# A linear-attention and expert-routing kernel: three double-bank PSUM buffers for the tile products, one bank shared by three small products, and a new set of step ranks

## The chip, the cores and the metric

The kernel runs on one core of one Trainium2 chip. The metric is the device time of one launch in microseconds (us). Before the change the median of three runs is 548.88 us.

## The reference, cut to what matters

Linear attention over 8 batches of 8 heads, 576 rows and 64 columns is followed by a norm over each head, a router of two levels (4 groups of 4 experts) and, for every one of the 4608 tokens, two matrix products by the one expert that was chosen.

```python
kv  = np.einsum('bhsd,bhse->bhde', k, v)
out = np.einsum('bhsd,bhde->bhse', q, kv)
rms = np.sqrt(np.mean(out * out, axis=-1, keepdims=True) + 1e-06)
x   = (out / rms * g_norm)          # then (4608, 512)
g_idx = np.argmax(x @ w_group, axis=1)
for g in range(4):                  # xg: the tokens of group g
    e_idx = np.argmax(xg @ w_expert[g], axis=1)
    for e in range(4):
        h  = np.maximum(xg[mask_e] @ w1[g, e], 0.0)
        ye = h @ w2[g, e]
        out[tok_idx] = (g_w * e_w)[:, None] * ye
```

## The kernel before, in words

The program has two stages. The first takes the queries, keys and values, makes the attention's output and sorts its rows by expert into a table in device memory (`xs`). The second takes the experts one after the other, largest first, in `for r in range(1, NE)`; the diff does not touch it.

The first stage works on 8 batches. For a batch b SyncE loads keys, values and queries (1 MB each; the last 64 rows of two batches come together as a "tail" of 256 KB). TensorE makes the state of a batch in `kv_product` (tile `kps`, line L567): 32 instructions for the main rows and 8 for the tail. Two copies take it out of PSUM (`kvd`, L555). `wide_product` multiplies it by the router's columns (tile `eps_`, L582, 8 instructions), and two copies put the result into `kvx` (L555), the widened state. From it `o_product` makes one tile of 128 rows at a time (tile `ops`, L615, two PSUM banks): four tiles for each batch and one tail tile for each two batches, 36 tiles, called c0 to c35 below; c31 to c34 are the last batch's and c35 is the last tail. ScalarE copies each tile out in two pieces (`o_keep`, `logits_keep`) and squares it. The tiles fall into 8 groups (of 3, 5, 5, 5, 6, 6, 4 and 2). When a group is complete, a chain of some 25 small VectorE steps (`route`) finds each token's expert. A product in the middle of that chain (tile `rk`, L834 to L840) counts the tokens before it; two VectorE steps read it (`kr` L846 and, in some groups, `lo` L1005). GpSimd then scatters the rows to `xs`.

After the fifth group the fullest expert is known well enough that work for it begins before the stage ends (`early_products`): for two blocks of 128 tokens, j = 0 and 1, a transpose (tile `xtr`, L1184), four pairs of layer-1 products (tile `l`, L369, n = 0 to 3), whose results ScalarE and VectorE split (`hhi` L1208, `hlo` L1214), and three passes of layer 2 (L1238) for each half hf of the output. The product `rv` (L1094) orders the experts once the last group is counted. Three of the four layer-2 sums, (j, hf) = (0,0), (0,1) and (1,0), are made here, and (1,1) opens the second stage.

What sets the order: every piece of work is a `step` with an engine, a rank and the steps that it needs. `give_out` lets each engine take, of the steps that can start by its own reckoning, the one of lowest rank. So each engine's instructions stand in a fixed order, which the tables at the top of the file (RANK, ROUTE, FOLD, LOADS, QLOADS, KVS, TAILS) shift. Where that reckoning leaves TensorE idle early on, `keep_warm` puts in products whose result nobody reads (tile `warm`, L463).

PSUM has eight banks. Before the change `kps`, `rk`, `eps_` (with `rv`) and the spare bank of `early_products` (with `warm`) have one each, and the tile products two buffers of two banks:

```python
ps_k = ph.enter_context(tc.tile_pool(name="ps_k", bufs=1, ...))
ps_r = ph.enter_context(tc.tile_pool(name="ps_r", bufs=1, ...))
ps_t = ph.enter_context(tc.tile_pool(name="ps_t", bufs=1, ...))
ps_e = ph.enter_context(tc.tile_pool(name="ps_e", bufs=1, ...))
ps_o = ph.enter_context(tc.tile_pool(name="ps_o", bufs=2, ...))
```

Of the kernel before, what the change touches and what calls it, by code (L numbers as in the profile page):

```python
# [9 lines left out]
F32 = mybir.dt.float32  # L10
# [30 lines left out]
RANK = {'wl0': 8653.7, 'wl3': -1621.61, 'hl': -1311.21, 'wh': -1318.76, 'wd': 837.56, 'ek': -5681.71, 'o': 3012.77, 'ok': -2407.34, 'sq': -1243.18, 'red': -1306.22, 'w': -1292.39, 'wl': 1177.39, 'wl2': -1202.9, 'xt': -7928.83, 'xs': -1359.19, 'l1': -1645.21, 'hs': -3081.53, 'l2': 3844.97, 'l3': -1942.42, 'l4': -2933.95, 'lk': -12.71, 'rd': -5685.6, 'l0': -1223.92, 'xp': 848.81}  # L41
ROUTE = [251.18, -2343.82, 3560.04, 792.99, -725.82, -1903.73, -9207.47, -3358.1]
FOLD = [242.46, -1256.85, -816.36, -1306.91, -3093.22, 8651.96, -1200.27, 1075.03]
LOADS = [-4110.76, -3081.87, -3084.03, -1307.74, -7.22, 49.97, 846.24, 4399.02]
QLOADS = [-2437.19, -1943.92, -1317.97, -1274.11, 651.34, 665.74, 1915.97, 6713.18]
KVS = [-2548.6, -1773.86, 3654.53, -1443.46, -3012.94, -39.98, -1312.76, -7927.08]
TAILS = [-3374.12, -1314.27, 191.74, -1649.28]
# [19 lines left out]
BIG = 11  # L67
CUT = 5

@with_exitstack  # L70
def tile_linattn_moe(ctx: ExitStack, tc: tile.TileContext, qm, qt, k, v, router, w1, w2, out):
# [345 lines left out]
    with ExitStack() as ph:  # L417
# [159 lines left out]
        def wide_product(b):  # L577
            kv["e"] = ps_t.tile([P, 512], F32, name="eps_", tag="pst")
# [21 lines left out]

        def o_product(c):
# [9 lines left out]
            ps = ps_o.tile([P, 2, 512], F32, name="ops", tag="pso")  # L611
# [84 lines left out]
        def tile_steps(c, nq):  # L696
# [3 lines left out]
            done["o", c] = step("PE", 1.24, c + RANK["o"], rdy + [get("o", c - 1), get("lk", c - 2)],  # L700
# [17 lines left out]
        def route(g):  # L718
# [45 lines left out]
            def f():  # L764
                nc.vector.scalar_tensor_tensor(out=tl([H], "nwy"), in0=v["nwa"], scalar=1.5, in1=v["y"], op0=ALU.add,
                                               op1=ALU.mult)
                v["rinv"] = v["nwy"].rearrange("p (t h) -> p t h", h=H)
# [961 lines left out]
```

## Time and profile before

| what | value |
|---|---|
| median of 3 runs | 548.88 us (548.83 to 552.87) |
| profiled execution, its own time | 550.13 us |
| span of the profile | 548.4 us, so 1.73 us lie outside of it |
| mean granted TensorE clock | 0.991 |
| TensorE busy in the span | 527.0 us (96%) |
| first stage, to the first product of (1,1) | 131.9 us |
| moved by DMA in the span | 126.27 MB |

PE is TensorE's matmul, PEld its weight loads, DVE is VectorE, ACT ScalarE, POOL GpSimd and SP SyncE. A line number is one of the kernel before. An fp32 product shows as two matmuls in the trace for one instruction in the program. PEclk is the clock that TensorE was granted, as a share of 2.4 GHz; 0.50 is 1.2 GHz. In a list of waits, "issue" means that the engine waited for nothing that the profile shows.

### The profile page before, as it was taken

To read this page: it belongs to the slowest core of one execution; us is meant where nothing else is said; L and a number is where in the kernel's file an instruction comes from. 1 tells how busy PE (TensorE), PEld (TensorE's weight loads), DVE (VectorE), ACT (ScalarE), POOL (GpSimd) and SP (SyncE) were. 2 spreads that over 40 slices of the span, in tenths; PEclk is the share of its full clock that TensorE was granted. 3 is DMA by queue.
4 is the path that set the end of the run, shared out by engine and by line. 5 is a ranking of instruction groups with operands and counts; after the bars stand their busy time and mean duration, and the time that the engine had idled before them with its cause. 6 is when DMAs were issued, how large, how long until landed. Compare 5 with 4: busy or idle time off the path is not lost.

```text
span 548.4 us, 11978 instructions
## 1 busy us (share of the span) xinstructions
PE 527.0 (96%) x4416; PEld 509.4 (93%) x4420; DVE 379.6 (69%) x800; ACT 275.2 (50%) x497; POOL 255.2 (47%) x244
## 2 busy tenths in 40 slices
PE   7999898988999999999999999999999999999994
PEld 5788787888999999999999999999999999999994
DVE  4158489792698777877676767776777778787750
ACT  1298487741554454545454545455454645455530
POOL 4001444663221146574746464645564554656543
PEclk9999799999999999999999999999999999999999
DMA  8999997566989373625855656474828474672001
GB/s 333 402 414 408 420 419 291 201 226 205 313 332 333 84 290 113 249 108 148 306 228 171 236 163 248 153 266 136 328 75 328 132 296 182 217 262 102 24 29 41
DMA packets 43631, 126.27 MB, mean 230 GB/s; under 512 B 6767, under 2 KB 25643, under 8 KB 32692
## 3 DMA queue, kind: packets, MB, share of 16 engines
q1 hardware_dynamic: 35732, 105.98, 53.3%
q0 software_dynamic: 7696, 19.48, 9.4%
q8 instruction: 35, 0.57, 0.4%
q14 instruction: 24, 0.20, 0.1%
q10 hardware_dynamic: 144, 0.04, 0.0%
HBM read 106.01 MB, written 20.38 MB: 230 GB/s over the span
## 4 chain that ended last, share of the span: by engine, by line
PE 88%; DMA 3%; SPq 2%; another core or an unknown queue 2%; issue 2%; ACT 1%; POOL 0%; POOLq 0%; ACTq 0%
PE ps L380 12%; PE ps L385 12%; PE ps L381 12%; PE psy L385 11%; PE psy L381 11%; PE psy L380 11%; PE ops L615 6%; PE l L369 3%; PE kps L567 3%; DMA tail_v<-in_v_dram 2%; SPq L542 2%; PE l L1238 1%; PE ps L369 1%; DMA tail_k<-in_k_dram 1%
## 5 line engine op out<-in xcount | busy, mean ns | idle before, releaser
L1417 POOL DMA_INDIRECT out_dram<-z,idx x138 | 166.2, 1204 | 169.1 <-DVE hhl L345 65.2
L385 PE MATMUL ps<-xh,wlo 128*128 128x364 f32 (+14 forms) x480 | 143.2, 298 | 0.0
L381 PE MATMUL ps<-xl,whi 128*128 128x364 f32 (+14 forms) x480 | 143.0, 298 | 0.0
L380 PE MATMUL ps<-xh,whi 128*128 128x364 f32 (+14 forms) x480 | 143.0, 298 | 0.0
L381 PE MATMUL psy<-hhl,w2h 128*128 128x364 f32 (+13 forms) x448 | 134.6, 300 | 0.0
L385 PE MATMUL psy<-hhl,w2l 128*128 128x364 f32 (+13 forms) x448 | 134.6, 300 | 0.0
L380 PE MATMUL psy<-hhl,w2h 128*128 128x364 f32 (+13 forms) x448 | 134.1, 299 | 0.0
L270 DVE TENSOR_TENSOR wlo<-wr,whi 128x1024 fp32r<-128x1024 f32 x64 | 90.7, 1418 | 24.2 <-ACT whi L266 24.1
L354 ACT CAST w2h<-wr 128x1024 fp32r<-128x1024 f32 x60 | 62.6, 1044 | 63.0 <-PE psy L381 44.2
L344 ACT ACTIVATE hhl<-ps 128x364 fp32r<-128x364 f32 (+14 forms) x120 | 50.5, 420 | 79.9 <-PE ps L385 74.6
L380 PEld LDWEIGHTS ps<-xh,whi 128*128 128x128 f32 x480 | 90.4, 188 | 0.0
L381 PEld LDWEIGHTS ps<-xl,whi 128*128 128x128 f32 x480 | 90.3, 188 | 0.0
L385 PEld LDWEIGHTS ps<-xh,wlo 128*128 128x128 f32 x480 | 90.3, 188 | 0.0
L385 PEld LDWEIGHTS psy<-hhl,w2l 128*128 128x128 f32 x448 | 84.5, 189 | 0.0
L381 PEld LDWEIGHTS psy<-hhl,w2h 128*128 128x128 f32 x448 | 84.5, 189 | 0.0
L380 PEld LDWEIGHTS psy<-hhl,w2h 128*128 128x128 f32 x448 | 84.5, 189 | 0.0
L358 DVE TENSOR_TENSOR w2l<-wr,w2h 128x1024 fp32r<-128x1024 f32 x60 | 73.3, 1221 | 14.2 <-ACT w2h L354 12.1
L287 POOL DMA_INDIRECT xs<-xo,keys x36 | 37.3, 1037 | 80.6 <-DVE s__814 L887 42.5
L345 DVE SCALAR_TENSOR_TENSOR hhl<-ps,hhl 128x364 fp32r<-128x364 f32 (+14 forms) x120 | 54.6, 461 | 18.2 <-ACT hhl L344 17.4
L266 ACT CAST whi<-wr 128x1024 fp32r<-128x1024 f32 x64 | 66.3, 1040 | 0.0
L1409 ACT ACTIVATE xh<-xt,rw 128x364 fp32r<-128x364 f32 (+14 forms) x60 | 32.6, 545 | 47.2 <-DVE xt L331 46.2
L1609 DVE STREAM_TRANSPOSE z<-psy 128x288 f32<-128x288 f32 (+3 forms) x56 | 28.4, 507 | 38.2 <-PE psy L385 28.0
(272 smaller groups left out, 636.6 us busy)
## 6 DMA issues: line engine op xcount, KB each, us to landing
wr<-in_w_dram SPq DMA_DIRECT2D x64, 1024.0 KB
m_k<-in_k_dram SPq DMA_DIRECT2D x7, 1024.0 KB
m_v<-in_v_dram SPq DMA_DIRECT2D x7, 1024.0 KB
m_q<-in_qm_dram SPq DMA_DIRECT2D x7, 1024.0 KB
xq<-xs SPq DMA_DIRECT2D x24, 136.0 KB
xq<-xs SPq DMA_DIRECT2D x20, 153.0 KB
out_dram<-z,idx POOLq DMA_INDIRECT x138
xq<-xs SPq DMA_DIRECT2D x12, 170.0 KB
```

The costliest lines, as they stand in the source:

```text
L266: nc.scalar.copy(out=hi, in_=w)
L270: eng.tensor_tensor(out=lo, in0=w, in1=hi.bitcast(F32), op=ALU.subtract)
L287: sc = nc.gpsimd.indirect_dma_start(out=xs, out_offset=bass.IndirectOffsetOnAxis(ap=keys[:, c:c + 1], axis=0), in_=x.rearrange("p i f -> p ...
L344: nc.scalar.activation(out=hh, in_=ps, func=AF.Relu)
L345: return nc.vector.scalar_tensor_tensor(out=hl, in0=ps, scalar=0.0, in1=hh.bitcast(F32), op0=ALU.max, op1=ALU.subtract)
L354: nc.scalar.copy(out=piece(hi, hf, i2), in_=halfpiece(wt[hf][0], i2))
L358: nc.vector.tensor_tensor(out=piece(lo, hf, i2), in0=halfpiece(wt[hf][0], i2), in1=piece(hi, hf, i2).bitcast(F32), op=ALU.subtract)
L380: nc.tensor.matmul(ps, lhsT=stat_h(c), rhs=mov_h(c), start=(c == 0), stop=False)
L381: nc.tensor.matmul(ps, lhsT=stat_h(c), rhs=mov_l(c), start=False, stop=False)
L385: nc.tensor.matmul(ps, lhsT=stat_l(d), rhs=mov_h(d), start=False, stop=(d == n - 1))
L615: nc.tensor.matmul(ops[c][lo:hi, pr, 0:XW], lhsT=qs[:, pr * step_ + at + lo:pr * step_ + at + hi], rhs=kx[:, pr, :], start=True, stop=True)
L1417: sc = nc.gpsimd.indirect_dma_start(out=out4, out_offset=bass.IndirectOffsetOnAxis(ap=idx[:, g:g + 1], axis=0), in_=z[:, g, :], in_offset= ...
```

## The change

The spare bank and the bank of `rk` go. The tile products get three fixed buffers of two banks (`ops0` to `ops2`), which tiles before c27 take in turn; from c27 on only the first two are used, and the third one's two banks serve the early products, beside the bank of `kps`. The eighth bank (`shared`) takes the widened state in columns 0 to 335, the ranks `rk` in 336 to 447 and `rv` in 448 to 511. All ranks are new. Filler products stop with the first tile that goes to the third buffer (c2), since they write there. One small tile of the router (`nwy`) gets a third buffer.

```diff
-RANK = {'wl0': 8653.7, 'wl3': -1621.61, 'hl': -1311.21, ...}
+RANK = {'wl0': 3934.31, 'wl3': -425.54, 'hl': -5452.75, ...}
...
+THREE = 27
...
-        ps_r = ph.enter_context(tc.tile_pool(name="ps_r", bufs=1, space=bass.MemoryType.PSUM))
-        ps_t = ph.enter_context(tc.tile_pool(name="ps_t", bufs=1, space=bass.MemoryType.PSUM))
-        ps_e = ph.enter_context(tc.tile_pool(name="ps_e", bufs=1, space=bass.MemoryType.PSUM))
-        ps_o = ph.enter_context(tc.tile_pool(name="ps_o", bufs=2, space=bass.MemoryType.PSUM))
+        ps_o = ph.enter_context(tc.tile_pool(name="ps_o", bufs=1, space=bass.MemoryType.PSUM))
+        shared = ps_o.tile([P, 512], F32, name="shared")
+        obufs = [ps_o.tile([P, 2, 512], F32, name=f"ops{i}") for i in range(3)]
...
-            kv["e"] = ps_t.tile([P, 512], F32, name="eps_", tag="pst")
+            kv["e"] = shared
...
+        def obuf(c):
+            return c % 3 if c < THREE else (c - THREE) % 2
+
+        def obuf_before(c):
+            return max([x for x in range(c) if obuf(x) == obuf(c)], default=-1)
...
-            ps = ps_o.tile([P, 2, 512], F32, name="ops", tag="pso")
+            ps = obufs[obuf(c)]
+            if obuf(c) == 2:
+                st["warm"] = None
...
-                                rdy + [get("o", c - 1), get("lk", c - 2)],
+                                rdy + [get("o", c - 1), get("lk", obuf_before(c))],
...
-                rk = v["rk"] = ps_r.tile([P, 512], F32, name="rk", tag="psr")
+                rk = v["rk"] = shared[:, 4 * HW:4 * HW + (GMAX + 1) * NE]
...
-                v["rv"] = ps_t.tile([P, 512], F32, name="rv", tag="pst")
+                v["rv"] = shared[:, 512 - 4 * NE:512]
...
-            free = {0: done["kk", B - 1], 1: []}
+            free = {0: done["kk", B - 1], 1: [done["lk", last3]], 2: [done["lk", last3]]}
...
-                return (ps_k, ps_e)[i].tile([P, 512], F32, name=nm, tag=("psk", "pse")[i])
+                return obufs[2][:, i - 1] if i else ps_k.tile([P, 512], F32, name=nm, tag="psk")
...
-                    i = (n + 1) % 2
+                    i = (n + 2) % 3
...
-                            t["o", hf] = ps_o.tile([P, 2, 512], F32, name="l2", tag="pso")
+                            t["o", hf] = obufs[obuf(NTL - 2 + hf)]
```

**TensorE's order around batch 5.** Before (`eps__906` and `eps__1001` are the widened states of batches 4 and 5):

```order
L615 MATMUL ops<-kvx_183,m_q 128x168 x16
L567 MATMUL kps<-tail_k,tail_v 64x64 x8
...
L582 MATMUL eps__906<-gw,kvd_185 64x84 x8
L567 MATMUL kps<-m_k,m_v 64x64 x32
L567 MATMUL kps<-tail_k,tail_v 64x64 x8
L615 MATMUL ops<-kvx_177,m_q 128x168 x4
L582 MATMUL eps__1001<-gw,kvd_186 64x84 x8
```

Of the change (ops_169 to ops_171 are the three buffers):

```order
L623 MATMUL ops_170<-kvx_178,m_q 128x168 x4
L623 MATMUL ops_171<-kvx_178,m_q 128x168 x4
L567 MATMUL kps<-m_k,m_v 64x64 x32
L567 MATMUL kps<-tail_k,tail_v 64x64 x8
L623 MATMUL ops_169<-kvx_178,m_q 128x168 x4
L582 MATMUL shared<-gw,kvd_181 64x84 x8
L623 MATMUL ops_170<-kvx_178,m_q 128x168 x4
```

The 32 main products of batch 5 stood behind c17, and now stand behind c14: three tiles of batch 3 (c15, c16 and the tail tile c17) moved behind them.

**TensorE's order around batch 7, the last.** Before:

```order
L615 MATMUL ops<-kvx_181,m_q 128x168 x12
L567 MATMUL kps<-m_k,m_v 64x64 x32
L567 MATMUL kps<-tail_k,tail_v 64x64 x8
L834 MATMUL rk<-base_b,ones_b 128x112
...
L840 MATMUL rk<-ohb,upper_b 128x96
L615 MATMUL ops<-kvx_181,m_q 128x168 x4
L582 MATMUL eps__1457<-gw,kvd_186 64x84 x8
...
L615 MATMUL ops<-kvx_183,m_q 128x168 x12
```

Of the change:

```order
L623 MATMUL ops_170<-kvx_176,m_q 128x168 x4
L842 MATMUL shared<-base_b,ones_b 128x112
...
L848 MATMUL shared<-ohb,upper_b 128x96
L567 MATMUL kps<-m_k,m_v 64x64 x32
L567 MATMUL kps<-tail_k,tail_v 64x64 x8
L582 MATMUL shared<-gw,kvd_181 64x84 x8
L623 MATMUL ops_169<-kvx_178,m_q 128x168 x4
```

The rank product of the fifth group and tile c30, which stood between the last state and its widening (before, three filler products follow that), now stand ahead of the state; nothing stands between the state's products and the widening.

**The end of TensorE's first stage.** Before:

```order
L1094 MATMUL rv<-perm,ones_k 128x64
L369 MATMUL l_1919<-xx,wr_1513 128x128 x8
L369 MATMUL l_1945<-xx,wr_1513 128x128 x8
L1238 MATMUL l_1720<-whi,hhi 128x256 x8
L1238 MATMUL l_1720<-whi,hlo 128x256 x8
L1238 MATMUL l_1720<-wlo,hhi 128x256 x8
L380 MATMUL ps<-whi,hhi 128x256
```

Of the change:

```order
L370 MATMUL ops_171<-xx,wr_1472 128x128 x16
L1102 MATMUL shared<-perm,ones_k 128x64
L1247 MATMUL ops_169<-whi,hhi 128x256 x8
L1247 MATMUL ops_170<-whi,hhi 128x256 x8
L1247 MATMUL ops_170<-whi,hlo 128x256 x8
L1247 MATMUL ops_170<-wlo,hhi 128x256 x8
L1247 MATMUL ops_169<-whi,hlo 128x256 x8
L1247 MATMUL ops_169<-wlo,hhi 128x256 x8
L381 MATMUL ps<-whi,hhi 128x256
```

The sum (0,1) stood wholly ahead of `rv`; now one of its passes stands between the last layer-1 product and the sum (1,0), and two behind it.

SyncE's order: in MB loaded ahead of it and with it, the tail of batches 2 and 3 ended at 10.25 of 27 before and ends at 8.5 now; the queries of batch 0, whole at 7.5 before, are whole at 8; keys and values of batch 3 end at 11.75 in place of 12.25, those of batch 4 at 14.75 in place of 15.5, those of batches 5 and 7 at 18 and 25.75 as before. A tail pair (of batches 4 and 5) stands between the two halves of the queries of batch 0.

## Rows read from the trace of the kernel before

**Rows 1.** The page, parts 1, 2 and 4: engines, slices and the chain

```profile
PE 527.0 (96%) x4416; PEld 509.4 (93%) x4420; DVE 379.6 (69%) x800; ACT 275.2 (50%) x497; POOL 255.2 (47%) x244
...
PEclk9999799999999999999999999999999999999999
...
PE 88%; DMA 3%; SPq 2%; another core or an unknown queue 2%; issue 2%; ACT 1%; POOL 0%; POOLq 0%; ACTq 0%
```

**Rows 2.** Busy time by stretch; the number ahead of PEld is PE's busy time

```profile
core 0: us, PE busy (x) PEld busy (x) DVE busy (x) ACT busy (x) POOL busy (x), PEclk, DMA share, GB/s
...
21.40:37.00 15.60, 15.03 (x177) 13.58 (x178) 5.19 (x8) 11.60 (x30) 0.00 (x0) 1.00 1.02 409
37.00:57.30 20.30, 20.19 (x318) 18.03 (x315) 17.25 (x59) 16.79 (x45) 4.12 (x4) 1.00 1.02 413
57.30:60.70 3.40, 1.31 (x15) 0.65 (x12) 1.39 (x5) 1.74 (x4) 2.01 (x2) 1.00 1.03 416
...
61.40:68.30 6.90, 6.90 (x56) 6.13 (x53) 1.24 (x6) 3.17 (x10) 1.95 (x2) 0.52 1.02 424
68.30:86.90 18.60, 17.64 (x206) 15.68 (x204) 16.68 (x72) 15.58 (x40) 7.20 (x7) 1.00 0.89 351
...
91.90:94.20 2.30, 0.62 (x4) 0.16 (x3) 2.16 (x5) 0.88 (x3) 2.14 (x3) 1.00 0.98 395
94.20:110.40 16.20, 15.25 (x126) 13.93 (x126) 12.49 (x36) 11.50 (x27) 10.43 (x11) 1.00 0.65 221
110.40:131.90 21.50, 18.26 (x157) 17.20 (x155) 14.09 (x66) 6.49 (x17) 11.39 (x14) 1.00 0.55 204
131.90:541.50 409.60, 408.61 (x2995) 407.41 (x2996) 296.55 (x494) 199.90 (x310) 207.88 (x156) 1.00 0.57 199
```

**Rows 3.** TensorE's timeline, 21 to 46 us: start, duration, what, idle before it

```profile
21.46 1.62 PE L567 MATMUL kps<-m_k,m_v 128*64 128x64 f32 x48
...
31.67 0.68 PE L567 MATMUL kps<-tail_k,tail_v 64*64 64x64 f32 x16 [0.47 <-DMA tail_v<-in_v_dram]
...
37.04 2.03 PE L567 MATMUL kps<-m_k,m_v 128*64 128x64 f32 x64
```

**Rows 4.** TensorE's timeline, 56 to 66 us and one full-speed widening

```profile
57.75 0.34 PE L567 MATMUL kps<-m_k,m_v 128*64 128x64 f32 x4 [0.40 <-issue]
...
61.80 1.12 PE L567 MATMUL kps<-tail_k,tail_v 64*64 64x64 f32 x16
...
65.38 1.39 PE L582 MATMUL eps__1001<-gw,kvd 64*64 64x84 f32 x16
...
80.70 0.80 PE L582 MATMUL eps__1251<-gw,kvd 64*64 64x84 f32 x16
```

**Rows 5.** Timelines around the last two batches: TensorE, ScalarE, VectorE

```profile
81.67 0.20 PE L840 MATMUL rk<-ohb,upper_b 128*128 128x80 bf16 x1
...
91.12 0.80 PE L582 MATMUL eps__1457<-gw,kvd 64*64 64x84 f32 x16
92.08 0.59 PE L463 MATMUL warm<-wide_b,ones_b 128*128 128x512 bf16 x2 [0.16 <-issue]
94.22 3.85 PE L615 MATMUL ops<-kvx,m_q 128*128 128x168 f32 x24 [1.54 <-ACT kvx L555]
...
81.54 0.88 ACT L555 COPY kvx<-eps__1251 64x336 f32<-64x336 f32 x2 [0.15 <-PE eps__1251 L582]
...
82.41 0.23 DVE L846 TENSOR_TENSOR kr<-rk,ohb 128x80 f32<-128x80 f32 x1
```

**Rows 6.** TensorE's timeline: an uncovered widening at 20 us; the end

```profile
18.38 0.68 PE L567 MATMUL kps<-tail_k,tail_v 64*64 64x64 f32 x16
...
19.98 0.80 PE L582 MATMUL eps__388<-gw,kvd 64*64 64x84 f32 x16 [0.38 <-DVE kvd L555]
...
112.75 0.51 PE L1238 MATMUL l<-whi,hhi 128*128 128x256 f32 x2 [1.41 <-issue]
...
129.04 0.50 PE L1238 MATMUL l<-whi,hhi 128*128 128x256 f32 x2 [1.14 <-ACT hhi L1208]
```

More of the change, by code (lines that the diff above doesn't have):

```diff
@@ L38 @@
 FIRST2 = [0, 0, 0, 0, 32, 0, 0, 24, 16, 0, 0, 4, 0, 0, 0, 0]
[L41 to L47, printed above, removed]
+RANK = {'wl0': 3934.31, 'wl3': -425.54, 'hl': -5452.75, 'wh': -1929.67, 'wd': -5528.13, 'ek': -2736.85, 'o': 88.66, 'ok': -2393.38, 'sq': -600.99, 'red': -4057.14, 'w': -2066.69, 'wl': -191.91, 'wl2': -1710.62, 'xt': -5351.9, 'xs': -1900.37, 'l1': 270.12, 'hs': -1890.94, 'l2': 772.57, 'l3': 1381.26, 'l4': -5463.72, 'lk': 0.43, 'rd': -422.75, 'l0': 8799.35, 'xp': -903.6}
+ROUTE = [-861.15, -4054.03, -2722.39, -4064.54, -908.72, 936.98, -7421.12, -225.98]
+FOLD = [-3581.41, 1257.42, 2478.29, 2590.43, -2425.86, 8579.54, 762.99, -2426.24]
+LOADS = [-4054.9, -4048.25, -2652.75, -1447.04, -1315.35, -958.49, 1249.14, 2567.26]
+QLOADS = [-1934.14, -1714.25, -1391.97, -1029.31, -135.35, 92.13, 2557.68, 2586.08]
+KVS = [2480.45, -855.89, -167.56, -425.72, -2362.71, -768.37, -2197.19, 2601.35]
+TAILS = [-4331.99, -1889.38, -5468.24, 2090.13]
 KEEP = ['DA', 'DA', 'AA', 'AA', 'AA', 'AA', 'AA', 'AA']
@@ L699, in tile_steps @@
                 done["ek", 2 * b] + done["ek", 2 * b + 1] + [done["tail", "q", b]])
-            done["o", c] = step("PE", 1.24, c + RANK["o"], rdy + [get("o", c - 1), get("lk", c - 2)],
+            done["o", c] = step("PE", 1.24, c + RANK["o"], rdy + [get("o", c - 1), get("lk", obuf_before(c))],
                                 lambda: o_product(c), give=1 if kind == "m" and j == NJ - 1 else 0)
@@ L764, in f @@
             def f():
-                nc.vector.scalar_tensor_tensor(out=tl([H], "nwy"), in0=v["nwa"], scalar=1.5, in1=v["y"], op0=ALU.add,
+                nc.vector.scalar_tensor_tensor(out=tl([H], "nwy", bufs=3), in0=v["nwa"], scalar=1.5, in1=v["y"], op0=ALU.add,
                                                op1=ALU.mult)
@@ L1162, in pair @@
                 return ps[:, 0:2 * P].rearrange("p (f t) -> p f t", f=2)
-            free = {0: done["kk", B - 1], 1: []}
+            last3 = max(c for c in range(NTL) if obuf(c) == 2)
+            free = {0: done["kk", B - 1], 1: [done["lk", last3]], 2: [done["lk", last3]]}
             hs, hhs, whs = {}, {}, []
             def bank(nm, i):
-                return (ps_k, ps_e)[i].tile([P, 512], F32, name=nm, tag=("psk", "pse")[i])
+                return obufs[2][:, i - 1] if i else ps_k.tile([P, 512], F32, name=nm, tag="psk")
             for j in range(HEAD // P):
@@ L1274, in tile_linattn_moe @@
                                                      mybir.EngineType.DVE, mybir.EngineType.Pool, SP}))
-        st["warm"] = ps_e.tile([P, 512], F32, name="warm", tag="pse")
+        st["warm"] = obufs[2][:, 1]
         for _ in range(32):
```

## The prediction

> **What bounds the kernel now.** I read the page first: TensorE is busy for 96% of the span, and the chain that ended last is TensorE's work for 88% of it [rows 1]. Nothing else can be the bound over the whole, so the question is where TensorE idles or runs slowly. The busy time by stretch answers it. In the second stage (131.9 to 541.5 us) TensorE rests for 409.60 - 408.61 = 0.99 us [rows 2], and the diff leaves that stage alone. What a change of the first stage can win is what TensorE loses between the first tile products and 131.9 us. Idle time by stretch is 0.57 (21.4 to 37.0), 0.11, 2.09 (57.3 to 60.7), 0.96, 1.68 (91.9 to 94.2), 0.95 and 3.24 us (110.4 to 131.9), 9.6 us together [rows 2]. To this comes the one slow stretch: from 61.4 to 68.3 us the granted clock is 0.52, that is the lower level of 1.2 GHz for nearly all of it, right behind the stretch in which TensorE was busy for only 1.31 of 3.40 us [rows 2]. The products show the price: the same 16 tail matmuls take 1.12 us there and 0.68 elsewhere, a widening 1.39 and 0.80 [rows 4, 6]. Lost: 6.90 x (1 - 0.52) = 3.3 us. So 12.9 us is all that could ever come back.
>
> The DMA engines are full up to about 68 us (share 1.02 in all three stretches [rows 2]), and 1 MB takes 1.05 MB / 0.41 MB per us = 2.56 us. TensorE waited for a load only once behind 21.4 us, for 0.47 us at 31.67 [rows 3]; from then on it is TensorE that is late, and the loads are ahead.
>
> One thing the rows do not show is a tile product that waits for a PSUM buffer: the only wait of one that stands out is for the copy of the widened state, 1.54 us [rows 5]. The third buffer therefore removes no wait by itself. What it changes is which order the planner may choose, and it is the orders that I price.
>
> **The change part by part.** The sum is made against the profiled execution, whose own time is 550.13 us (span 548.4 and 1.73 around it). The median shown, 548.88, is 1.25 us below.
>
> *Loads and the first tiles: -0.6.* The tail that TensorE waited for stands at 8.5 MB in place of 10.25, so it lands (10.25 - 8.5) x 2.56 = 4.5 us earlier, and the 0.47 us go. From the state of batch 2 (21.46) to that of batch 3 (37.04) 15.58 us pass [rows 3], of which 0.57 are idle [rows 2]. Work is the same, so batch 3 may start 0.6 us earlier; its values now end at 11.75 MB, some 5.25 x 2.56 = 13.4 us behind those of batch 2 (6.5 MB, 21.46 us), at 34.9 us, so they do not hold it. The tail pair of batches 4 and 5 must wait on SyncE's queue until batch 1's state is made (18.38 + 0.68 = 19.06 [rows 6]); queued behind it are the second half of batch 0's queries and everything later. The loads ahead of it end 0.5 MB behind those of 21.46 us, at 22.7, so the queue still has 3.6 us of work when the wait ends. I take nothing for it. Bounds: -0.6, and +1.4 if a whole 0.5 MB (1.3 us) came late.
>
> *The state of batch 5: -1.0.* Before, its main products stopped five times for 0.4 to 0.5 us, with nothing named as the reason, and the slow stretch followed [rows 2, 4]. They are the shortest matmuls of the stage. Batches 2, 3, 4 and 7 made the same 64 without such stops; batch 6 had two, inside the 0.96 us idle of 68.3 to 86.9 [rows 2]. The change makes as many of these runs, three tiles earlier for batch 5, under the same load on the DMA engines. So I cannot call the stops gone: I take half of the 2.09 us, with bounds of 0 and -2.09. Whether the clock then falls is priced apart. It fell after 2.09 us of rest in 3.40, not after 1.68 in 2.30 or 0.96 spread over 18.6. In the likeliest case the stage keeps one slow stretch, at the old place or another: 0, with bounds of -3.3 and +3.3.
>
> *The state of batch 7: +0.9.* Before, the rank product and tile c30 stood between the state and its widening and covered the copies of the state. Now nothing does. The row for this is the widening of batch 1: its state ended at 19.06, it began at 19.98 (a filler product lies between), so 0.92 us [rows 6]. Tile and rank product only move, so their own time cancels. Behind the widening, c31 waits as before: 94.22 - 91.92 = 2.30 us from the end of the widening, 0.59 of it filler [rows 5], which goes, for nothing. Bounds: +0.38, the idle alone of that row, and +2.30, the longest wait for such copies.
>
> *The early products: -1.1.* Sum (1,0) waited for the last split result of layer 1, 1.14 us [rows 6]. Now one pass of sum (0,1) stands between; 16 matmuls of 256 columns, about 1 us, cover it. Sum (0,0) starts right behind the fourth pair of layer 1 as before and should wait its 1.41 us [rows 6] again. Three banks in place of two spare TensorE nothing: it waited for a free bank nowhere but perhaps in the 0.95 us of 94.2 to 110.4 [rows 2]. Bounds: -1.5 and 0.
>
> *One bank for three products: +0.1.* Ranks and widened state now exclude each other where they used to overlap: the rank product at 81.67 to 81.87 ran while ScalarE read the widened state from 81.54 to 82.42 [rows 5]. Where the rank product stands right behind the widening, as here, TensorE goes on, ScalarE's copies start some 0.3 us later, and VectorE's `kr`, at 82.41 before, is at the end of the copies anyway. Only the first rank product stands one tile behind a widening: copies of 0.88 us behind a tile of some 1.3 us leave it about 0.1 us to wait. The next widening waits for VectorE to have read the ranks, which it did at once in that row. Bounds: 0 and 0.88 at each of three places, 2.6.
>
> The Trainium skill (PSUM — Partial Sum Buffer, section "PSUM bank collisions raise a hardware error") says that the compiler puts a dependency between any two instructions on different engines that touch the same bank and quadrant, reads included, whichever columns they touch. By that rule the first bank shared by `rk` and the widened state costs up to the 2.6 us above (549.8 in all); by the trace of before alone, which has the two in banks of their own and overlapping, it costs nothing (547.1). No run so far shows it.
>
> Sum: -0.6 - 1.0 + 0 + 0.9 - 1.1 + 0.1 = -1.7 us, so 548.4 for an execution like the profiled one and 547.2 for the median.
>
> **What is late next.** The second stage needs the last group's ranks. The tail tile c35 stood behind three pairs of layer 1 before, and stands ahead of all of them now, so its chain of VectorE steps runs beside some 6 us more of products. That chain does not become the bound unless TensorE gains over 6 us.
>
> **The rivals.**
>
> *The clock never falls (A).* The stops of batch 5 came in a run of products that now stands elsewhere; if they do not come back, what preceded the fall of the clock is gone. Then the 3.3 us go and perhaps the other half of the stops: -1.7 - 3.3 = -5.0 to -6.0, so 542.9 to 543.9, 543.4. For it: all other rests of the stage were followed by a full clock [rows 2]. Against it: two of six such runs had stops, and the uncovered widening is new.
>
> *The clock falls behind the last state (B), the slower side.* Around the state of batch 7 TensorE now rests 0.92 us, widens for 0.80 and rests up to 2.30: 3.2 us idle of 4.0, more than before the slow stretch of the profile. If the clock falls there as well, the last tiles and the first pairs of layer 1 run at half speed, +3.3; and if batch 5 keeps all its stops, +1.0: -1.7 + 4.3 = +2.6, so 551.5. The point from which it decides is a second row of granted clock near 0.5 between 88 and 105 us. For it: the rest is the stage's longest. Against it: the same place with 1.68 us of rest kept its clock [rows 2].
>
> *The shared bank holds TensorE (C).* If a widening or a rank product waits for a read by another engine at three places for 0.88 us each, the gain is gone: -1.7 + 2.6 = +0.9, so 549.8. For it: VectorE reads the third group's ranks twice, and the second read (`lo`) stands far behind the first. Against it: TensorE has six tiles and a state between that rank product and the next widening.
>
> **How the numbers follow.** Forecast 0.50, A 0.20, B 0.15, C 0.15. The forecast's own range is 545.0 to 549.3 (the bounds of the stops, the early products and the loads). The range of 8 in 10 reaches to the lower half of A and nearly all of B: 543.0 to 551.9. A measurement of this kernel tells about 1% from no change, 5.5 us. Faster by that, below 543.4, needs half of A (0.10) and the forecast's last 0.03: 0.13. Slower, above 554.4, needs B with the bank's waits on top, a third of B and some of C: 0.07. The rest, 0.80, is within 1%.
>
> **What would show it.** In the profile of the changed kernel the first product of (1,1) should come 1 to 3 us earlier than at 131.9; no tile product or tail state should wait for a load behind 21 us; the widening of batch 7 should start some 0.9 us behind its state; and the wait of 1.14 us for a split result should be gone. Step by step it would be wrong if the early loads came late (idle before 37 us above 0.57), if widenings waited for VectorE, or if the slow stretches numbered none or two. The whole is wrong if the time lies outside 543.0 to 551.9, or if the second stage loses more than its 1 us of rest.

## The result and the profile after

The changed kernel takes 551.38 us (median of 22 runs) beside 547.67 us of the kernel before (22 runs on the same chip): a ratio of 1.0071, 95% interval 1.0057 to 1.0085. It is 3.7 us slower, a difference under 1% but clear of the noise, where 1.7 us less was forecast. The profiled execution took 552.82 us (span 551.1), 2.7 us more than the one of before.

The runs come in sets; what shares a set shares a chip and its own runs of the kernel before. The sets show two pictures, and no number below can be read without that: in three sets the kernel before takes 547.7 to 549.3 us, in three others 538.7 to 539.1. I call the first three disturbed, for the reason that the traces give further down. The ratio above is from a disturbed set.

The page of the changed kernel, parts 1 and 2, answers to [rows 1]:

```profile
PE 527.5 (96%) x4417; PEld 510.7 (93%) x4417; DVE 378.1 (69%) x800; ACT 275.1 (50%) x497; POOL 255.5 (46%) x244
...
PEclk9999799999999999999999999999999999999999
```

Nothing is to be seen there: TensorE's busy time and the clock by slices are those of before. The loss is in a few places of the first stage. Busy time by stretch of the changed kernel (columns as in [rows 2]):

```profile
54.00:59.00 5.00, 2.72 (x29) 1.85 (x31) 4.43 (x12) 0.82 (x3) 3.31 (x3) 0.86 1.01 411
59.00:65.00 6.00, 6.00 (x47) 5.34 (x46) 0.00 (x0) 2.44 (x7) 1.95 (x2) 0.55 1.01 417
...
90.00:95.00 5.00, 3.45 (x80) 2.75 (x76) 4.55 (x26) 3.59 (x10) 1.96 (x4) 1.00 0.99 335
95.00:99.00 4.00, 4.00 (x16) 4.00 (x17) 2.97 (x8) 1.36 (x3) 3.17 (x3) 0.57 0.55 204
99.00:112.00 13.00, 9.51 (x85) 8.53 (x84) 8.62 (x25) 8.48 (x22) 8.10 (x9) 1.00 0.59 194
112.00:135.70 23.70, 21.24 (x182) 20.17 (x181) 14.89 (x69) 6.98 (x17) 11.43 (x13) 1.00 0.46 174
135.70:545.00 409.30, 408.64 (x2996) 407.30 (x2996) 295.47 (x494) 200.19 (x311) 208.91 (x157) 1.00 0.58 201
```

The second stage is as full as before (0.66 us idle). The state of batch 5 again rests 2.28 us between 54 and 59, and a slow stretch comes with it (0.55 of full clock from 59 to 65; in the trace's record of the clock it runs from 57.6, while the state still stops, to 64.4); a second one (0.57, with 3.4 us at the lower level of 1.2 GHz) is new, right behind the rest of 1.55 us around the state of batch 7; and 3.49 us are idle between 99 and 112. TensorE's timeline names them:

```profile
37.53 2.04 PE L567 MATMUL kps<-m_k,m_v 128*64 128x64 f32 x64
...
57.01 0.37 PE L567 MATMUL kps<-m_k,m_v 128*64 128x64 f32 x5 [0.37 <-issue]
...
92.85 1.18 PE L582 MATMUL shared<-gw,kvd 64*64 64x84 f32 x16 [0.47 <-ACT kvd L555]
95.00 6.85 PE L623 MATMUL ops<-kvx,m_q 128*128 128x168 f32 x32 [0.97 <-issue]
101.69 0.60 PE L1193 MATMUL ops<-ident,xx 128*128 128x128 f32 x4
102.22 1.36 PE L623 MATMUL ops<-kvx,tail_q 128*64 128x168 f32 x16
...
103.81 0.20 PE L848 MATMUL shared<-ohb,upper_b 128*128 128x96 bf16 x1
107.13 2.05 PE L370 MATMUL ops<-xx,wr 128*128 128x128 f32 x16 [3.12 <-ACT xx L1198]
...
116.66 0.88 PE L1247 MATMUL ops<-whi,hhi 128*128 128x256 f32 x4 [1.09 <-issue]
```

Four tiles take 6.85 us in place of the 5.28 that they need at full clock (the run fill below), and the first product of layer 1 waits 3.12 us for ScalarE's copy of the turned tokens. The odd thing is that copy. The four transposes end at 102.29, ScalarE has nothing else to do from 102.72 on, and yet (its timeline):

```profile
102.13 0.59 ACT L628 COPY xo<-ops 128x512 f32<-128x512 f32 x1
106.39 0.69 ACT L1198 ACTIVATE xx<-ops,rw 128x512 f32<-128x512 f32 x1 [3.67 <-remote]
```

"remote" means that the profile has no releaser. In the trace's record of semaphore changes, TensorE's signals for the transposes, for the tail tile (ended 103.58) and for the ranks (ended 104.01) all arrive between 106.36 and 106.62, 2.6 to 4.1 us late. The profile models the end of a product, but here the products behind the transposes had already started (102.22, 103.51), so the signal was late and not the work. What goes on at that time is on GpSimd's timeline, a run of nine scatters from 93.18 to 105.18, and the state of batch 5 has one beside it too:

```profile
52.67 0.97 POOL L288 DMA_INDIRECT xs<-xo,keys  x1 [0.38 <-ACT xr L555]
...
55.23 1.41 POOL L288 DMA_INDIRECT xs<-xo,keys  x1 [0.30 <-issue]
...
102.93 0.97 POOL L288 DMA_INDIRECT xs<-xo,keys  x1 [0.30 <-issue]
104.21 0.97 POOL L288 DMA_INDIRECT xs<-xo,keys  x1 [0.30 <-issue]
```

The kernel before had the same company at its five stops (57.35 to 60.69), which the prediction did not look at:

```profile
57.47 1.03 POOL L287 DMA_INDIRECT xs<-xo,keys  x1 [0.30 <-issue]
58.81 0.97 POOL L287 DMA_INDIRECT xs<-xo,keys  x1 [0.30 <-ACT kvx L555]
```

It had late signals too. The widening of its last batch ended at 91.92 [rows 5], and its signal is recorded at 93.26; tile c34 ended at 99.65. ScalarE's copies of the two, with scatters from 90.34 to 92.60 and from 93.95 to 102.89 beside them:

```profile
93.29 0.88 ACT L555 COPY kvx<-eps__1457 64x336 f32<-64x336 f32 x2 [1.47 <-PE eps__1457 L582]
...
102.67 0.59 ACT L620 COPY xo<-ops 128x512 f32<-128x512 f32 x1 [2.17 <-PE rk L840]
```

From here came the theories: S, signals of TensorE come late beside GpSimd's scatters; P, its short state products stop beside them; F, the rest around the state of batch 7 brings the second slow stretch. Their rivals are in the expectations.

### The profile page after: what moved, and what is told of

Read it like the earlier page. It is cut to its first block, busy times and chain, and to the rows that moved or that the text cites. A ratio compares the mean times of both kernels' runs of the same rounds, so it can differ in the third digit from the quotient of the medians.

```text
span 551.1 us, 11960 instructions
## 1 busy us (share of the span) xinstructions
PE 527.5 (96%) x4417; PEld 510.7 (93%) x4417; DVE 378.1 (69%) x800; ACT 275.1 (50%) x497; POOL 255.5 (46%) x244
## 5 line engine op out<-in xcount | busy, mean ns | idle before, releaser
L271 DVE TENSOR_TENSOR wlo<-wr,whi 128x1024 fp32r<-128x1024 f32 x64 | 88.6, 1384 | 23.7 <-ACT whi L267 23.7
L288 POOL DMA_INDIRECT xs<-xo,keys x36 | 38.5, 1069 | 85.4 <-DVE s__802 L895 43.1
```

The costliest lines, as they stand in the source:

```text
L271: eng.tensor_tensor(out=lo, in0=w, in1=hi.bitcast(F32), op=ALU.subtract)
L288: sc = nc.gpsimd.indirect_dma_start(out=xs, out_offset=bass.IndirectOffsetOnAxis(ap=keys[:, c:c + 1], axis=0), in_=x.rearrange("p i f -> p ...
```

## The experiments

**One break in the run of scatters (hold22).** The scatter of tile c22 also waits for the copy (`turned` is ScalarE's first copy of turned tokens); no engine's order changes.

```diff
+LATE = [22]
...
+        if c in LATE:
+            data_dep(sc, kv_ends["turned"])
...
+                    if j == 0:
+                        kv_ends["turned"] = a
```

> The changed kernel, in which the scatter of tile c22 on GpSimd's queue waits until ScalarE has copied the first transposed token block (xx, line 1198 of the changed kernel); all other orders are the same. In the changed kernel the transposes end at 102.29 us, but ScalarE's copy starts at 106.39, so the first product of layer 1 waits 3.12 us. Theory S (TensorE's signal that the transposes are done arrives late, because GpSimd prepares scatters one behind the other from 93.2 to 105.2 us): with the pause behind c21 the copy starts between 102.3 and 103.2 us, the 3.12 us shrink below 0.6, and the time is 2.5 to 3.2 us under the changed kernel's 551.4 (548.2 to 548.9; ratio to before 1.001 to 1.002). Rival R1 (ScalarE's copy waits for something of its own, a transfer whose buffer it takes or a step ahead of it): the copy still starts near 106.4 us and the time stays at 551.4, or is 0.5 to 1 us longer because the scatters behind c22 come later.

Measured: 551.22 us, ratio 1.0042 (1.0027 to 1.0056) beside a before of 549.3, so not the 548.2 to 548.9 asked for. The copy came as theory S says. TensorE:

```profile
103.26 0.60 PE L1196 MATMUL ops<-ident,xx 128*128 128x128 f32 x4
...
111.00 3.84 PE L373 MATMUL ops<-xx,wr 128*128 128x128 f32 x32 [1.78 <-DVE hlo L1230]
...
116.68 0.88 PE L1254 MATMUL ops<-whi,hhi 128*128 128x256 f32 x4 [1.36 <-ACT hhi L1224]
```

ScalarE's copy:

```profile
104.04 0.71 ACT L1201 ACTIVATE xx<-ops,rw 128x512 f32<-128x512 f32 x1
```

and GpSimd's scatters, c21 and the held c22:

```profile
102.21 0.97 POOL L289 DMA_INDIRECT xs<-xo,keys  x1 [0.30 <-issue]
105.03 0.97 POOL L289 DMA_INDIRECT xs<-xo,keys  x1 [1.85 <-ACT xx L1201]
```

In the pause the copy starts 0.18 us behind the transposes (103.86), and the 3.12 us are gone. That is one execution, and the hold is not proved by it: in a later disturbed set (after_c, below) the unedited kernel has the copy in time as well. R1 falls by both, since the same copy, with the same steps ahead of it, does not wait there. In hold22 the gain does not reach the end: the slow stretch lasted 6.8 us in this execution (95.0 to 101.8), and signals beside the scatters that were pushed back came late instead (1.78 us at 111.00, 1.36 at 116.68). The first product of (1,1) starts at 135.76; in the changed kernel at 135.74.

**Filler around the state of batch 7 (fill).** The filler writes to a bank of the third buffer, which tiles from c27 on do not use.

```diff
+            if c == 29:
+                st["warm"] = obufs[2][:, 1]
```

> The changed kernel with filler products given back between the state of batch 7, its widening and tile c31 (six of 512 columns, 0.3 us each; the changed order has none behind its first tiles). In the changed kernel TensorE rests 0.47 and 0.97 us there, and from 95.1 to 98.5 us the granted clock is 0.5. Theory F (the rest brings the clock down): the second slow stretch goes, tiles c31 to c34 take 5.2 us in place of 6.85, and the time falls by 1.0 to 1.7 us, to 549.7 to 550.4, unless the later wait for xx (3.12 us) grows by what is won, since its end is then set by GpSimd's run of scatters at 105.2 us: then the slow stretch goes and the time stays at 551.4. Rival R2 (the clock falls for what the batch did before, not for the rest behind it): the slow stretch stays and the time is the same or up to 0.8 us longer by the filler itself.

Measured: 551.03 us, 1.0043 (1.0028 to 1.0059). TensorE:

```profile
95.49 5.28 PE L625 MATMUL ops<-kvx,m_q 128*128 128x168 f32 x32 [0.66 <-ACT kvx L555]
...
105.88 0.27 PE L370 MATMUL ops<-xx,wr 128*128 128x128 f32 x1 [1.17 <-issue]
```

The slow stretch is gone, the four tiles take 5.28 us, and part of it goes to stops inside the layer-1 product, again beside scatters; the execution's first stage ends at 133.84. Over all profiles with the changed order, disturbed or not, the clock fell within 4 us of the end of the state of batch 7 in 5 of 9 without filler and in 0 of 4 with it. If filler did nothing, none in 4 would still come up about once in ten such draws, so F is a tendency and R2 is not ruled out. Neither run had the changed kernel itself in its set, so what they are worth in us is open.

**Only the ranks, only the buffers.** ranks_only is the kernel before with the seven new tables, buffers_only the changed kernel with the seven old ones.

> The kernel before with the changed kernel's seven tables of ranks, and its own PSUM buffers (two for tile products, banks of their own for widened states, ranks and row values). The planner gives another order than in either kernel, with tile c34 behind the ranks and a layer-1 product between, and filler around the widening of batch 7. If the loss lies in what the new order brings about at one place (late xx, rest without filler), most of it is gone here: 0.995 to 1.003 of before. If the ranks as such lose (loads first, batch 7 late), 1.004 to 1.008 as the whole change.

> The changed kernel with the seven tables of ranks of before: three double-bank buffers and the shared bank stay. If sharing the bank or the two banks lost to the early products cost the 3.7 us, the ratio to before is 1.004 to 1.010, and widenings or rank products wait for VectorE or ScalarE for over 1 us in total. If the banks are free of cost and the order decides, it lies within 0.997 to 1.004, unless the order that the planner finds for it meets a late signal of its own, which a wait of over 1 us behind a run of scatters would show.

Measured: ranks_only 552.03 us, 1.0058 (1.0039 to 1.0078); buffers_only 561.21 us, 1.0233 (1.0198 to 1.0268). ranks_only lies where the ranks as such were to lose (1.004 to 1.008), without a shared bank or a third buffer; buffers_only is slower than either of its two cases. The parts do not add up to the whole, since the planner makes another order of each. In buffers_only two of the longest waits are these:

```profile
101.45 2.60 PE L623 MATMUL ops<-kvx,m_q 128*128 128x168 f32 x8 [3.32 <-ACT xr L555]
...
125.36 0.69 PE L1102 MATMUL shared<-perm,ones_k 16*128 16x64 f32 x2 [4.05 <-DVE perm L1095]
```

The first row waits for a copy of logits, which stood on ScalarE behind two weight casts (98.55 to 100.57); such waits come to 5.1 us at three places. In the plan such a copy frees a tile's buffer, so a wait for a tile buffer is not excluded here. The second row waits for its own input (`perm`) and not for the bank that it shares, and so do the other waits of widenings and rank products (for `kvd` and `ohb`). ranks_only has one thing of use: its state of batch 5 falls into a pause of GpSimd, has no stop, and no slow stretch follows before 100 us. Its state of batch 6, beside 2.24 us of scatters, stops four times (1.62 us).

**The scatters moved off the state of batch 5 (hold_b5), and of batch 6 (hold_b56, with filler hold_b56_fill).** TensorE's order in hold_b5 is that of the changed kernel, instruction for instruction; the scatters of c2 and c3 wait, and those of c4 and c5 behind them in GpSimd's order. hold_b56 has the entry `8: 6` as well.

```diff
-HOLD = {2: 4, 3: 4, 6: 5, 13: 6, 15: 7}
+HOLD = {2: 5, 3: 5, 6: 5, 13: 6, 15: 7}
```

> The changed kernel in which the scatters of tiles c2 to c5 wait for the state of batch 5 instead of batch 4 (the table that holds scatters back: 2 and 3 to batch 5). TensorE's order is the same, instruction for instruction. In the changed kernel GpSimd prepares scatters for 4.34 us of the state of batch 5 (52.28 to 59.89 us), and the state stops seven times, 2.59 us; the granted clock is 0.5 for 6.83 us from there on. Theory P (TensorE's short state products stop while GpSimd prepares scatters, and this rest takes the clock down): at most two stops are left (those beside c0 and c1), together under 0.7 us, the slow stretch behind goes, and the state of batch 6 starts 4 to 5.5 us earlier than at 75.16; of that 2 to 5 us reach the end, since loads, the scatters behind and the late signals of the early products may take some back: 546.4 to 549.4. Rival R3 (the stops come with the fetch of TensorE's instructions or with the load on the DMA engines, and the scatters beside them are chance): the stops stay at 2 to 2.6 us, the slow stretch too, and the time is 551.4 plus or minus 0.7.

> As hold_b5, and the scatters of tiles c8 to c12 wait for the state of batch 6 as well. The planner then moves a rank product into the state of batch 7 and the one of tile group 4 ahead of the last tail tile, and turns the first token block behind them. Theory P: the states of batches 5 and 6 have no stop beyond those next to c0 and c1 (1.22 us of batch 6 go too), no slow stretch before 90 us; 1 us less than hold_b5 up to the state of batch 7. Behind it scatters are packed more densely (c8 to c23 follow one another), so late signals cost there: 545.5 to 549.5. Rival R3: both states stop as before, 551.4 plus or minus 1.

> As hold_b56, with filler products between the state of batch 7 and the early products. By theories P and F there is no slow stretch at all, which alone is worth 1.7 us where hold_b56 has one behind batch 7, and nothing (or the filler's own 0.3 to 0.9 us) where it has none: 545 to 549.

> The changed kernel once more, unedited, on the chip of the three runs beside it: a ratio to before of 1.0057 to 1.0085 by the first measurement; its stops, slow stretches and the late copy of xx are to come back at the same places if they belong to the program and not to one execution.

This set was an undisturbed one: before 538.73; hold_b5 540.45 (1.0025, 0.9999 to 1.0051), hold_b56 543.27 (1.0080, 1.0058 to 1.0101), hold_b56_fill 543.07 (1.0072, 1.0051 to 1.0093), the changed kernel 539.56 (1.0035, 1.0005 to 1.0065). No theory could be tried here, since in none of the four traces does a state stop or a signal come late in more than one case, scatters beside it or not. The expected times (545 to 549.5, a ratio of 1.0057 to 1.0085 for the changed kernel) were those of a disturbed set and do not apply. That the changed kernel shows neither stops nor a late copy here says, by its expectation, that they do not belong to the program alone. hold_b56 loses by its own order: its transposes wait 2.98 us for VectorE at 97.10, which after_again has nowhere. The two intervals above 1.000 of the changed kernel here and below (1.0035 and 1.0038) say that it loses a little without any disturbance as well.

**Both kernels, hold_b5 and a mended version in one set.** mended is hold_b5, fill and hold22 together.

> The kernel before, unedited, as a control beside the three runs that follow. Two chips have given two pictures: on one (before at 547.7 to 549.3 us) TensorE's signals came late and its state products stopped while GpSimd prepared scatters; on the other (before at 538.7) neither was seen in any of four kernels. Theory C (what GpSimd's scatters cost TensorE depends on the chip and not on the order of the kernel): the picture is one of these two whole, ratio 0.998 to 1.002; at about 538 us the state of batch 5 has no stop, no granted clock of 0.5 before 100 us, and the first product of (1,1) starts between 120 and 123 us; at about 548 us stops of 2 us and one slow stretch of 6.8 us return. Rival: the two pictures come from the kernels, then this one shows stops at 538 us too.

> The changed kernel, unedited, beside before_c. On a chip where GpSimd's scatters disturb: 1.0057 to 1.0085, xx about 3 us late, two slow stretches. On one where they do not: 1.000 to 1.006, no wait for xx; what is left is the uncovered widening of batch 7 (0.47 and 0.97 us) and the waits of the early products.

> hold_b5 again (the scatters of c2 to c5 wait for the state of batch 5, order of TensorE unchanged). On a disturbed chip theory P asks for at most two stops at batch 5 (under 0.7 us of 2.6), no slow stretch behind it, and 2 to 5 us less than after_c; R3 asks for no difference. On an undisturbed chip there is nothing to win: within 0.5 us of after_c.

> The changed kernel with hold_b5, fill and hold22 together: scatters c2 to c5 behind the state of batch 5, c22 behind the first turned block, filler around the widening of batch 7. On a disturbed chip, by theories P, S and F together, no slow stretch before 130 us and no wait for xx: 3 to 7 us under after_c and under before (ratio 0.990 to 0.999), less what the early products lose to signals that come late beside scatters pushed back. On an undisturbed chip: within 1 us of after_c, as filler and holds have nothing to save there and cost up to 1 us.

A disturbed set: before 549.32 and before_c 549.63 (1.0004, 0.9987 to 1.0020), the changed kernel 551.13 (1.0027, 1.0011 to 1.0044), hold_b5_c 549.00 (0.9996, 0.9979 to 1.0012), mended 549.08 (0.9997, 0.9966 to 1.0028). The changed kernel stopped seven times in batch 5 (2.85 us) as in its first profile. The late copy did not come back, though: its profile (an execution of 555.60 us, 4.5 above its median) has three slow stretches, 17.1 us together, and this (all engines):

```profile
106.61 0.60 PE L1193 MATMUL ops<-ident,xx 128*128 128x128 f32 x4
...
107.44 0.69 ACT L1198 ACTIVATE xx<-ops,rw 128x512 f32<-128x512 f32 x1
...
111.04 0.96 PE L370 MATMUL ops<-xx,wr 128*128 128x128 f32 x7 [1.04 <-issue]
```

The copy starts 0.23 us behind the transposes, beside scatters that were not held, and the first layer-1 product stops inside instead. So the 3.12 us belong to one execution and not to the order alone. TensorE of hold_b5_c:

```profile
51.75 2.08 PE L567 MATMUL kps<-m_k,m_v 128*64 128x64 f32 x64
...
61.71 0.30 PE L623 MATMUL ops<-kvx,m_q 128*128 128x168 f32 x1 [0.32 <-issue]
```

and GpSimd beside it:

```profile
61.64 0.97 POOL L288 DMA_INDIRECT xs<-xo,keys  x1 [0.31 <-issue]
```

With the same products in the same order, the state runs through in 2.08 us once no scatter stands beside it, and the stops turn up ten us later in tile products, where the scatters now are. mended shows the same (its state of batch 5 takes 2.09 us). So that the scatters beside the stops are chance, as R3 has it, falls; P holds, and the disturbance goes where the scatters go. By what path a scatter stops TensorE is open; a fetch of instructions that scatters delay would look the same. hold_b5_c wins 2.1 us over the changed kernel (each of its ten runs, 548.66 to 550.37, lies below each of the eleven of the changed kernel, from 550.40 on) and no more than ties with before; a slow stretch of 6.8 us (64.4 to 71.2) comes with the stops. mended does no better, 2 us under the changed kernel where 3 to 7 were expected. Its profiled execution took 555.72 us, 6.6 above its median, so that its trace says little of the median: it has no slow stretch before 100 us but two behind (101.2 to 104.6 and 118.3 to 121.7), and new waits of 1.88 and 2.36 us of tile products for ScalarE's copies (at 97.95 and 101.72), beside scatters that were pushed back.

**Both kernels in undisturbed sets.**

> The kernel before, unedited, as the control with a profile of its own: 0.998 to 1.002. On a chip where GpSimd's scatters disturb TensorE (before near 548), the first product of (1,1) at 131 to 133 us; on one where they do not (near 538), at 120 to 123 us without a stop in any state.

> The changed kernel, unedited, on the same chip. Disturbed chip: 1.002 to 1.008 of before, with stops in the states of batches 5 and 6, and either xx late (over 1 us of wait ahead of the first layer-1 product) or stops inside that product. Undisturbed chip: 1.000 to 1.004, all of what is left then belongs to the order itself (tails loaded first, uncovered widening of batch 7).

> hold22 again, now beside the unedited changed kernel on one chip. Theory S': the late signal is real, but the later step (the split result of the fourth layer-1 pair, also late beside scatters) sets the end of the first stage, so holding c22 gives back 0 to 0.8 us. Theory S (the 3.12 us are on the path to the end): 2.5 to 3.2 us less than after_d. On an undisturbed chip: equal to after_d within 0.5 us.

> hold22 with the filler around the widening of batch 7. If the rest there brings the second slow stretch (theory F), no row of granted clock near 0.5 between 88 and 110 us, and 0.5 to 1.7 us less than hold22_d where that one has such a row; if the later step of theory S' sets the end, under 0.5 us less. On an undisturbed chip: equal to after_d, or longer by the filler's own 0.3 us.

> The changed kernel, unedited, as the control of the run beside it. On an undisturbed chip (before near 539) 0.999 to 1.003, as after_d; on a disturbed one (before near 548) 1.002 to 1.008.

> hold22 with the filler around the widening of batch 7, again. On a disturbed chip: 1.5 to 4 us less than after_e if the late copy xx (3.12 us) and the second slow stretch (1.7 us) are what reaches the end; within 0.8 us of after_e if a later late signal (the split result of the fourth layer-1 pair) sets the end of the first stage, and then the stops in the state of batch 5, which hold_b5_c took away for 2.1 us, are what the change loses there. On an undisturbed chip: within 1 us of after_e, as before.

Two sets, both undisturbed. First: before_d 538.84 (0.9997, 0.9981 to 1.0012), the changed kernel 539.42 (1.0011, 0.9992 to 1.0030), hold22_d 539.11 (1.0019, 0.9989 to 1.0049), hold22_fill 538.74 (1.0003, 0.9989 to 1.0016). Second: the changed kernel 539.80 (1.0038, 1.0013 to 1.0063), hold22_fill_e 539.09 (1.0019, 0.9991 to 1.0046). So hold22 and filler tie with the changed kernel, as asked for there, and what they are worth in a disturbed set stays open. TensorE of the changed kernel in the last set:

```profile
51.95 2.08 PE L567 MATMUL kps<-m_k,m_v 128*64 128x64 f32 x64
...
85.19 5.28 PE L623 MATMUL ops<-kvx,m_q 128*128 128x168 f32 x32 [0.97 <-ACT kvx L555]
90.31 0.60 PE L1193 MATMUL ops<-ident,xx 128*128 128x128 f32 x4
...
92.47 2.01 PE L370 MATMUL ops<-xx,wr 128*128 128x128 f32 x16
...
121.06 0.39 PE L381 MATMUL ps<-whi,hhi 128*128 128x256 f32 x1 [0.46 <-ACT xx L1268]
```

GpSimd beside it:

```profile
52.33 0.97 POOL L288 DMA_INDIRECT xs<-xo,keys  x1 [0.37 <-ACT xr L555]
...
90.97 0.98 POOL L288 DMA_INDIRECT xs<-xo,keys  x1 [0.31 <-DMA xs<-xo,keys]
```

and ScalarE's copy of the turned tokens:

```profile
91.00 0.76 ACT L1198 ACTIVATE xx<-ops,rw 128x512 f32<-128x512 f32 x1
```

The same kernel, the same scatters beside the same state: 64 products in 2.08 us without a stop, the copy 0.1 us behind the transposes, no wait ahead of layer 1. And the kernel before (before_d) reaches the same point at the same time:

```profile
55.87 2.08 PE L567 MATMUL kps<-m_k,m_v 128*64 128x64 f32 x64
...
85.22 3.85 PE L615 MATMUL ops<-kvx,m_q 128*128 128x168 f32 x24 [0.22 <-ACT kvx L555]
...
121.08 0.39 PE L380 MATMUL ps<-whi,hhi 128*128 128x256 f32 x1 [0.46 <-ACT xx L1259]
```

That is the fastest of the changed kernel's three undisturbed profiles; the others reach it at 122.70 and 123.26, the last with a slow stretch right behind the state of batch 7 (85.9 to 89.4).

## Why the prediction was wrong

The first product of (1,1) was to come 1 to 3 us earlier than at 131.9; it came at 135.74, 3.8 us later. That is more than the 2.7 us by which the two profiled executions differ; what lies behind it is 1.1 us shorter in the one of the changed kernel. The terms, as forecast and as this one profile has them:

| term | forecast | measured |
|---|---|---|
| loads and first tiles (state of batch 3) | -0.6 | 37.53 - 37.04 = +0.5 |
| stops of batch 5 | -1.0 | 2.59 - 2.09 = +0.5 |
| stops of batch 6 | none counted | 1.21 - 0.94 = +0.3 |
| slow clock | 0 | a second stretch, 3.4 x 0.5 = +1.7 |
| state of batch 7, idle | +0.9 | (0.47 + 0.97) - (0.16 + 1.54) = -0.3 |
| early products, idle | -1.1 | 5.95 - 4.19 = +1.8 |
| shared bank | +0.1 | 0 |

Measured they sum to +4.5, and the filler that went (0.59 us) takes them to 3.9, near the 3.8. For the early products it is the idle time from 99 us on against that from 94.2 on [rows 2]. The largest misses are the early products (by 2.9 us), the slow clock (1.7) and the stops of batch 5 (1.5). They have one step in common: the forecast took the waits in the rows of before as properties of TensorE's order, and did not ask what GpSimd did beside them. The second disturbed profile of the changed kernel splits its loss otherwise (first product of (1,1) at 138.28, three slow stretches, no wait for xx), so these sizes are those of one execution.

*Stops of batch 5.* The step that failed is "So I cannot call the stops gone: I take half of the 2.09 us". The half rested on a count of runs with and without stops, and the count had a cause that stood in the rows: [rows 2] show GpSimd busy for 2.01 of the 3.40 us. In disturbed sets every state with over 1.8 us of scatters beside its main products stopped (14 of 14, at least 0.9 us each); with 0.4 to 1.0 us beside it 5 of 10 stopped once, for 0.2 to 0.3 us, and from batch 3 on none without scatters did. The 1.8 us are in part made by the stops, since a state that runs through is over in 2.1 us. The new order has 4.4 us of scatters beside the main products of batch 5, against 3.0 before. Moving them off was worth 2.1 us in hold_b5_c; but the kernel before pays for its own five stops, and the difference between the two kernels is 0.5 us.

*Early products.* That the 1.14 us would go came true, and sum (0,0) waited again (1.09 for 1.41). What failed is that these were the only waits the term looked at. Behind the transposes stand, in the new order, the tail tile and a rank product, 1.7 us of cover, which is enough in an undisturbed trace (no wait at 92.47) and not enough for a signal that comes 4 us late. In the old order a signal that came 3 us late hit tile c34 (ended 99.65, copied from 102.67), whose copy nothing on TensorE needed at once.

*Slow clock.* "In the likeliest case the stage keeps one slow stretch" failed; the mechanism of rival B came true at its place (95.1 to 98.5 us at 0.5), at half the price that I gave it (1.7 for 3.3 us), and with a rest of 1.55 us where B counted 3.2. I had priced the filler behind batch 7 at nothing; with filler the stretch did not come in 4 profiles, and in 4 of 9 it did not come without.

*State of batch 7.* That the widening now waits for the copies was right and the size off: 0.47 us, near the lower bound of 0.38, not 0.92. That "c31 waits as before" failed, and the gain of 0.3 is luck: the wait of before was no price of the order, since its copy began 1.37 us behind the widening for a late signal. Tile c31 now waits 0.97, about the 0.88 that the copies take. Undisturbed the term has the sign that was forecast: 0.22 us idle before (before_d) and 0.47 + 0.97 after (after_e), +1.2.

*Loads.* The 0.47 us wait of the tail went, as forecast, and more was lost ahead of it: the first tails are loaded ahead of the halves of batch 0, so the first state starts at 8.84 in place of 7.68. From the state of batch 2 to that of batch 3 it is 14.92 us (22.61 to 37.53) in place of 15.58, the 0.6 that was forecast; the start of batch 2, 1.15 us later than before, is what the term left out. In the other profiles with the changed order the state of batch 3 starts between 36.7 and 38.2 us, so the loss of 0.5 is within their scatter.

*Shared bank.* Right: no rank product waits for a bank, and the widenings wait for their own input alone (`kvd`, 0.38 us at batch 1 as before and 0.47 at batch 7). By the rule of the Trainium skill (PSUM — Partial Sum Buffer, section "PSUM bank collisions raise a hardware error") up to 2.6 us had been possible; the run shows none of it on the path. Rival C falls.

*The range* of 543.0 to 551.9 held the median shown. The forecast's own range, 545.0 to 549.3, is narrower than the bounds that it names: added up they reach from 545.7 to 551.3.

In the undisturbed sets the forecast gain fails as well: the ratios there are 1.0011 to 1.0038. Of what the forecast counts on, before_d has 0.17 us of the wait for a tail and nothing else: no stop, no slow stretch, no wait for a split result.

How much of the loss the disturbance makes is open. The ratios of disturbed sets (1.0071 and 1.0027) and of undisturbed ones (1.0035, 1.0011 and 1.0038) overlap, and so do their intervals. The traces show the stops, the late signals and the second slow stretch at their places, and an experiment shows what moving the scatters off the state of batch 5 is worth to the changed kernel (2.1 us). The shares of the late copy and of the slow stretch in the difference between the two kernels are argued.

## What to carry to other kernels

When a matmul run stops "for nothing", or a consumer starts long after its producer has ended, look at what every other engine does in that stretch, in the same window, before giving it a chance of half. An order that a planner finds is only as good as the signal times it assumes: a chain of short steps between engines (product, copy, product) needs cover for a late signal, or must not stand beside a run of scatters. And measure in more than one set of runs: the same two kernels differ by 0.7% in one set and by 0.1% in another.

## What the runs showed of the hardware

*Late signals and stops beside scatters, in some sets only.* Counted up to 140 us, by the first semaphore change recorded from the end of each signalled product of TensorE on: in the ten disturbed profiles it comes more than 0.25 us behind the end for 113 of 216 products that end while GpSimd prepares a scatter, and for 7 of 481 with no scatter within 0.4 us; in the ten undisturbed profiles for 2 of 247 beside a scatter. The disturbed profiles hold 745 changes for 784 such products, and a product whose own change is missing counts as late, so some of the late ones may be of that kind. The copies shown above are late by ScalarE's own rows. The two kinds of set differ by most of 10 us in the first stage alone: the first product of (1,1) starts at 131.9 and 131.5 in two disturbed profiles of the kernel before and at 121.1 in the undisturbed one, and for the changed kernel at 135.7 and 138.3 against 121.1 to 123.3.

*The disturbance outlasts the scatter's row.* In the kernel before the last scatter beside the state of batch 5 ends at 59.78, and the last stop runs from 60.20 to 60.69. The Trainium skill (Perfetto Trace Analysis, section "DMA Instruction — SWDGE (GPSIMD)") says that the profiled end of such an instruction is the end of descriptor generation and not of the data's movement. The stop behind the row fits that, and no run here tests it: preparing and moving were not told apart, and no kernel without the scatters was run.

*What makes a set disturbed is open.* One chip number stands for a set at 549.3 and for one at 538.7, so the number does not decide it, nor does the kernel.
